# A fused S5 scan and GEGLU kernel on one core: a new hand-over order of its 692 steps

## The chip, the core and the metric

The kernel runs on one core of a Trainium2 chip. The core has five engines, each with its own instruction stream: TensorE (PE in the profile, its weight loads PEld), VectorE (DVE), ScalarE (ACT), GpSimd (POOL) and SyncE (SP), which in this kernel issues nearly all DMAs. Engines wait for each other only through semaphores. The metric is the device time of one execution in microseconds (us), and of several executions the median. Lower is better.

## The reference

The input `x` has 2048 tokens of 512 features. It is normalised, goes through a complex diagonal recurrence (S5) and, beside it, through a gated feed-forward net; the two results are multiplied and added to the input. All inputs and the output are bf16.

```python
def _A_ref(x, Lambda_re, Lambda_im, B_re, B_im, C_re, C_im, log_dt, Dskip):
    Lam = Lambda_re + 1j * Lambda_im                  # 512 states
    dt = jnp.exp(log_dt)
    Lam_bar = jnp.exp(dt * Lam)
    B_bar = ((Lam_bar - 1.0) / Lam)[:, None] * Bmat   # 512 x 512
    Bu = jnp.einsum("bld,pd->blp", x + 0j, B_bar)
    for t in range(L):                                # 2048 tokens
        h = Lam_bar[None, :] * h + Bu[:, t, :]
        hs.append(h)
    y = 2.0 * jnp.einsum("blp,dp->bld", hseq, Cmat).real + x * Dskip[None, None, :]

def _B_ref(x, w_gate, w_up, w_down):                  # 512 -> 1376 -> 512
    return (_gelu(x @ w_gate) * (x @ w_up)) @ w_down

xn = _layernorm(x, axis=-1)
s = _A_ref(xn, ...)
g = _silu(_B_ref(xn, ...))
return x + s * g
```

## The kernel before

**Tiling.** The tokens are cut into four slabs of 512, each slab into four token tiles of 128 (m = 0 to 3). The 512 features are four row tiles of 128 (k = 0 to 3), over which a matmul group accumulates in a PSUM bank. The 1376 hidden columns of the feed-forward net are cut into 512, 512 and 352 (c = 0, 1, 2). The 512 complex states are four tiles, worked on in two halves.

**What is done for a slab.** `norm` normalises it (ScalarE) and transposes it into `xnT` by a DMA. `gate_tile` (matmuls L536, ScalarE evacuations L539) makes the up and the gate products of a token tile, six groups of four matmuls; `gated` (L518, VectorE, two instructions, of 1024 and 352 columns) multiplies the two into `at`, and `at_t` transposes `at` by a DMA. `half` makes the drive of two state tiles: four groups of matmuls with `BT` (L615), evacuated by ScalarE into `U` (L617); VectorE rotates it (L627, a product over 4096 columns into `Q`), sums the products (L639, 2048 columns), runs four scans (L646) and rotates and sums back into `hst`. `down_pair` makes the down projection (L564, 11 matmuls of 512 columns a tile) and its SiLU. `y_tile` puts the skip term into a bank (L575, ScalarE), accumulates eight matmuls of `hst` with C on it (L579), multiplies by the gate (L585, `yg`), adds the input (L586, `ot`) and stores. The slabs are interleaved, so that matmuls of one slab lie beside the scans of another.

**The head.** Slab 0 is begun while weights still arrive. Its tiles are centred (L418 and L424, VectorE) and transposed on TensorE (`head_t`: L387 for tile 0 in two halves, L400 for the others, evacuated at L402 into `xcT`, which lies in the buffer `W`). Then `up_rows` (L462) multiplies one token tile with one row tile and one 512-column chunk of the up weights as soon as that piece has landed, one matmul a step; `first_w` (L499) makes a group of four matmuls, with the 352-column piece of the up weights or with the gate weights. `parameters` transposes the S5 parameters on TensorE; from them come the time step, the angles and the rotation tables.

**The loads.** SP issues them in the head one after another: the four x tiles (steps 0, 1, 2, 7; 128 KB each), the up weights in halves of a row tile (3 and 4 for row 0, 5 and 6 for row 1, 8 and 9 for row 2; 128 KB each; 10 for row 3, 256 KB), the 352-column up piece of all rows (11, 352 KB), gate columns 512 to 1375 (12, 864 KB), gate columns 0 to 511 (13, 512 KB). Behind them come x slab 1 (151), D (154), the two transposes into `BT` (14, 15, L314), slab 0's transpose into `xnT` (175, L436), the down weights (152, 1280 KB, and their 96 KB tail 153), x slabs 2 and 3 (295, 438) and the C transposes (220, 221).

**What sets the order.** The program adds 692 steps to a `Plan`, numbered as they are added, each with its engine, the steps it depends on and the buffers it holds. `Plan.run` emits them in the order of the hand-written tuple `ORDER` (L21 to L46), and the instructions are not reordered after that: each engine runs its own steps in that order, and a wait holds everything behind it on the same engine. `SLOTS` (L47 to L89) says which physical buffer or PSUM bank every group uses: `ps` are banks 0 to 5, `pp` banks 6 and 7, and the other names are the buffers of `SIZES`. The costs that the steps carry in the code are not used when the plan runs.

The steps that the prediction names, with their lines:

| steps | engine | what |
|---|---|---|
| 71 | PE | `up_rows(1, 0, 0)`, L462: first matmul of token tile 1 |
| 86, 97 / 90, 92, 94 / 101 | PE | `up_rows` of chunk 1: tile 0, rows 2 and 3 / tile 3, rows 0 to 2 / tile 1, row 3 |
| 115 | PE | `first_w` of tile 2 with the 352-column up piece, L499 |
| 129 | PE | `first_w` of tile 1 with gate columns 512 to 1023, L499 |
| 205 | PE | slab 0, `half`: first group with the second half of `BT`, L615 |
| 396; 397, 399 | PE; ACT | slab 2, `half`: first drive group; evacuations of the first two into `U` |
| 404, 405, 411 | DVE | slab 2: rotation L627, sum L639, rotation back |
| 457, 402, 609, 611, 613 | PE | groups of `gate_tile` (L536) or `half` (402, L615), each of which refills a bank |
| 483, 503, 504, 524, 525 | DVE | gated products of slab 2, L518 (503 and 524: 1024 columns) |
| 515 | ACT | evacuation of an up group, L539 |
| 507, 678 | PE | `y_tile`, L579: a slab 1 tile, and the first of slab 3 |
| 535 | DVE | `yg` product of a slab 1 tile, L585 |
| 554, 570 | DVE | slab 3: the sums that write the two halves of `hst`, L639 |

Of the kernel before, what the change touches and what calls it, by code (L numbers as in the profile page):

```python
# [18 lines left out]


ORDER = (  # L21
# [24 lines left out]
)  # L46
SLOTS = {  # L47
# [4 lines left out]
    ),  # L52
    "pp": (
        0, 1, 0, 1, 0, 1, 0, 1, 0, 0, 0, 1, 0, 1, 0, 1, 0, 1, 0, 1, 1, 0, 1, 0, 1, 1, 1, 0, 0, 0, 0, 1, 1, 0, 1, 0, 1, 0, 1,
    ),
    "U": (
        0, 1, 0, 2, 0, 1, 0, 2,
    ),
    "g2": (
        5, 0, 1, 4, 3, 0, 4, 2, 2, 0, 1, 5, 3, 1, 4, 5,  # L60
    ),
    "at": (
        2, 0, 1, 3, 2, 1, 0, 0, 0, 1, 2, 3, 2, 3, 0, 1,
    ),
    "gtA": (
        0, 0, 1, 1, 0, 1, 0, 1, 1, 0, 0, 0, 1, 1, 0, 0,
    ),
    "gtB": (
        1, 1, 0, 0, 0, 0, 1, 1, 1, 0, 0, 0, 0, 1, 0, 1,
    ),  # L70
    "ubA": (
        0, 1, 0, 0, 1, 1, 1, 0, 0, 0, 1, 1,
    ),
    "ubB": (
        0, 0, 1, 1, 1, 0, 0, 1, 0, 0, 1, 0,
    ),
    "yg": (
        0, 0, 1, 1, 0, 1, 0, 1, 0, 1, 1, 0, 0, 0, 1, 0, 1, 0,
    ),
    "ot": (  # L80
        1, 1, 1, 0, 1, 0, 0, 0, 0, 0, 0, 1, 1, 0, 1, 0, 1,
    ),
    "sk": (
        2, 3, 0, 1, 5, 7, 4, 6, 0, 1, 3, 2, 5, 4, 6, 7,
    ),
    "atT": (
        0, 1, 3, 0, 1, 1, 3, 2, 0, 3, 2, 1, 1, 2, 3, 0,
    ),
}  # L89

# [829 lines left out]
```

## Time and profile before

| | |
|---|---|
| median of 3 runs | 179.1 us (178.98 to 179.23) |
| the profiled execution, its span | 176.9 us |
| TensorE busy | 172.1 us, 97% of the span |
| VectorE busy | 154.6 us, 87% |
| ScalarE busy | 132.6 us, 75% |
| GpSimd busy | 10.9 us, 6% |
| DMA | 18.66 MB, mean 105 GB/s |
| chain that ended last | TensorE 94% of the span, DMA 2% |

The span is what the instructions of one execution cover, from the first to the last. The device time is longer by what lies around it: the median is 2.2 us above the span shown. Busy shares are averages over the whole span; the chain that ended last is followed back from the last instruction to what released each step, and tells which engine or load held the end up. A row of a view gives start and length in us, the engine, the line, the operation with its output and input buffers, the shapes, and, in brackets, how long the engine was idle just before and what released it. `SPq` is a DMA that SP has issued. An instruction's length is its own duration; on VectorE and ScalarE consecutive ones overlap a little.

### The profile page before, as it was taken

To read this page: it belongs to the slowest core of one execution; us is meant where nothing else is said; L and a number is where in the kernel's file an instruction comes from. 1 tells how busy PE (TensorE), PEld (TensorE's weight loads), DVE (VectorE), ACT (ScalarE), POOL (GpSimd) and SP (SyncE) were. 2 spreads that over 40 slices of the span, in tenths; PEclk is the share of its full clock that TensorE was granted. 3 is DMA by queue.
4 is the path that set the end of the run, shared out by engine and by line. 5 is a ranking of instruction groups with operands and counts; after the bars stand their busy time and mean duration, and the time that the engine had idled before them with its cause. 6 is when DMAs were issued, how large, how long until landed. Compare 5 with 4: busy or idle time off the path is not lost.

```text
span 176.9 us, 2418 instructions
## 1 busy us (share of the span) xinstructions
PE 172.1 (97%) x834; PEld 82.3 (47%) x849; DVE 154.6 (87%) x253; ACT 132.6 (75%) x246; POOL 10.9 (6%) x25
## 2 busy tenths in 40 slices
PE   8999999999999999999999999999999999999992
PEld 2554544454454444444444444444444444444451
DVE  3743799999999988999999699999999999999343
ACT  6679999989999999956697665735898860793310
POOL 2640500000200000011000000000000000000000
PEclk9999999999999999999999999999999999999999
DMA  5999999997092730040057050063007300550531
GB/s 150 285 347 247 160 288 189 305 217 158 8 193 43 138 62 4 0 82 0 0 115 150 2 111 0 0 126 70 0 11 154 87 0 4 129 123 0 113 119 30
DMA packets 48467, 18.66 MB, mean 105 GB/s; under 512 B 40296, under 2 KB 48328, under 8 KB 48456
## 3 DMA queue, kind: packets, MB, share of 16 engines
q1 hardware_dynamic: 48432, 18.52, 46.7%
q8 instruction: 6, 0.10, 0.2%
q14 instruction: 5, 0.04, 0.1%
q10 hardware_dynamic: 24, 0.00, 0.0%
HBM read 6.46 MB, written 2.10 MB: 48 GB/s over the span
## 4 chain that ended last, share of the span: by engine, by line
PE 94%; DMA 2%; SPq 1%; issue 1%; DVE 0%
PE bank L536 31%; PE bank L564 21%; PE bank L615 16%; PE bank L579 16%; PE bank L499 7%; PE bank L462 3%; DMA wu<-in_B_w_up_dram 2%; SPq L296 1%; SPq L287 0%; DVE yg L585 0%; DVE ot L586 0%; PE bank L400 0%
## 5 line engine op out<-in xcount | busy, mean ns | idle before, releaser
L536 PEld LDWEIGHTS <-xnT 128*128 128x128 bf16 x288 | 28.1, 98 | 29.4
L564 PE MATMUL bank<-wd,atT 128*128 128x512 bf16 (+1 forms) x174 | 40.2, 379 | 0.1
L536 PE MATMUL bank<-wu,xnT 128*128 128x512 bf16 (+1 forms) x140 | 31.9, 356 | 0.1
L536 PE MATMUL bank<-wg,xnT 128*128 128x512 bf16 (+1 forms) x139 | 31.7, 356 | 0.3
L615 PE MATMUL bank<-xnT,BT 128*128 128x512 bf16 x128 | 30.9, 379 | 0.1
L646 DVE TENSOR_TENSOR_SCAN Fs<-rho,ini,W 128x512 bf16<-128x512 f32 x24 | 29.8, 1272 | 0.1
L579 PE MATMUL bank<-C,hst 128*128 128x512 bf16 (+1 forms) x134 | 29.7, 366 | 0.1
L564 PEld LDWEIGHTS <-atT 128*128 128x128 bf16 (+1 forms) x176 | 17.2, 98 | 20.3
L539 ACT ACTIVATE ubA<-bank 128x512 bf16<-128x512 f32 x24 | 14.6, 614 | 8.8 <-PE bank L536 8.3
L617 ACT ACTIVATE U<-bank 128x512 bf16<-128x512 f32 x32 | 19.1, 622 | 1.7 <-PE bank L615 1.7
L579 PEld LDWEIGHTS <-hst 128*128 128x128 bf16 x136 | 13.3, 98 | 14.0
L615 PEld LDWEIGHTS <-BT 128*128 128x128 bf16 x128 | 12.5, 98 | 14.3
L627 DVE TENSOR_TENSOR Q<-U,tab 128x4096 bf16<-128x4096 bf16 x8 | 18.3, 2287 | 0.7 <-ACT tab L715 0.6
L539 ACT ACTIVATE gtA<-bank 128x512 bf16<-128x512 f32 x24 | 14.8, 616 | 5.3 <-PE bank L536 4.6
L627 DVE TENSOR_TENSOR Q<-Fs,tab 128x4096 bf16<-128x4096 bf16 x8 | 18.3, 2285 | 0.1
L567 ACT ACTIVATE g<-bank 128x512 f32<-128x512 f32 x16 | 9.2, 594 | 12.1 <-PE bank L564 12.1
L585 DVE TENSOR_TENSOR yg<-bank,g 128x512 bf16<-128x512 f32 (+1 forms) x17 | 11.1, 655 | 5.0 <-PE bank L579 4.6
L539 ACT ACTIVATE ubB<-bank 128x352 bf16<-128x352 f32 x12 | 5.7, 475 | 6.6 <-PE bank L536 5.5
L838 ACT ACTIVATE junk<-x_tok 128x512 bf16<-128x512 bf16 x16 | 10.2, 649 | 0.0
L499 PE MATMUL bank<-wg,W 128*128 128x512 bf16 (+1 forms) x47 | 9.7, 356 | 0.1
L843 ACT ACTIVATE xna<-x_tok,nb,rs 128x512 bf16<-128x512 bf16 x12 | 9.6, 876 | 0.0
L575 ACT ACTIVATE bank<-sk 128x512 f32<-128x512 bf16 (+1 forms) x17 | 9.5, 577 | 0.1
(121 smaller groups left out, 190.0 us busy)
## 6 DMA issues: line engine op xcount, KB each, us to landing
out_dram<-ot SPq DMA_DIRECT2D x15, 128.0 KB, 1.8
x_tok<-in_A_x_dram SPq DMA_DIRECT2D x3, 512.0 KB, 5.6
wd<-in_B_w_down_dram SPq DMA_DIRECT2D x1, 1280.0 KB, 7.1
wg<-in_B_w_gate_dram SPq DMA_DIRECT2D x1, 864.0 KB
wu<-in_B_w_up_dram SPq DMA_DIRECT2D x6, 128.0 KB, 3.3
x_tok<-in_A_x_dram SPq DMA_DIRECT2D x4, 128.0 KB, 2.2
wg<-in_B_w_gate_dram SPq DMA_DIRECT2D x1, 512.0 KB, 7.8
wu<-in_B_w_up_dram SPq DMA_DIRECT2D x1, 352.0 KB, 3.9
```

Source lines behind the costliest of these rows:

```text
L499: T.matmul(ps[:, 0 : b - a], lhsT=xcT[:, k, m * P : (m + 1) * P], rhs=wt[:, k, a:b], start=(k == 0), stop=(k == KT - 1))
L536: T.matmul(ps[:, 0 : b - a], lhsT=xnT[:, s % 2, m, k, :], rhs=wt[:, k, a:b], start=(k == 0), stop=(k == KT - 1))
L539: acts(b - a, lambda: act(out=dst, in_=ps[:, 0 : b - a], func=AF.Copy if up else AF.Gelu_apprx_tanh), [key], [ok], table=None if up else " ...
L564: T.matmul(ps[:], lhsT=atT[:fs, k, iT * P : (iT + 1) * P], rhs=wd[:fs, k, :], start=(k == 0), stop=(k == NFT - 1))
L579: T.matmul(ps, lhsT=hst[s % 2][:, j // NPT, j % NPT, m * P : (m + 1) * P], rhs=C2[:, j // NPT, j % NPT, c0:c1], start=False, stop=(j == 2 ...
L585: dve(w, lambda: V.tensor_tensor(out=yg[iy][:, 0:w], in0=ps, in1=g2[ig][:, c0:c1], op=ALU.mult), [key, ("g2", gg)], [("yg", gy)])
L615: T.matmul(ps[:], lhsT=BT[:, ri, k, pt * P : (pt + 1) * P], rhs=xnT[:, s % 2, :, k, :], start=(k == 0), stop=(k == KT - 1))
L617: acts(512, lambda q=q, ri=ri, ps=ps: act(out=U[ui][:, ri, q, :], in_=ps[:], func=AF.Copy), [key], [("U", ug, q, ri)])
L627: dve(4096, lambda: V.tensor_tensor(out=Qf, in0=src.unsqueeze(1).to_broadcast(WQ), in1=table, op=ALU.mult), reads, ["Q"], rate=2.0)
L646: pl.add(DVE, 1.12 if s == 0 else 1.185, lambda ri=ri, q=q, pt=pt, first=first: V.tensor_tensor_scan(out=Fs[:, ri, q, :], data0=rho[:, pt ...
L838: acts(512, lambda i=i, fn=fn, sc=sc, m=m: act(out=junk()[:], in_=x_tok[:, s * M + m, :], func=fn, scale=sc, accum_out=sx[:, s, i, m : m + ...
L843: acts(512, lambda m=m: act(out=xn[m], in_=x_tok[:, s * M + m, :], func=AF.Identity, scale=rs[:, s, m : m + 1], bias=nb[:, s, m : m + 1]), ...
```

## The change

The steps are the same 692, with the same work in each. What changes is `ORDER`, the order in which they are emitted, and `SLOTS`, which buffer each group uses. Both tuples are replaced as a whole.

In the head SP issues both halves of row tile 1 of the up weights (6, 5) and token tile 3 (7) ahead of the 352-column piece (11), which was issued ahead of all three. The transposes of the parameters (38) come right behind the first pair of transposes of token tile 0, and were four steps later on TensorE; their cast on VectorE (39) moves with them. TensorE's order up to the gate weights is another one. The queues, as the tuples give them:

```
SP before: 0 1 2 3 4 11 6 7 5 8 10 9 12 13 151 154 14 175 15 295 153 438 248 152 221 176 177 220 371 178
SP after:  0 1 2 3 4 6 5 7 11 8 10 9 12 13 151 154 14 175 153 15 295 248 438 177 152 220 221 176 178 179

PE before: 29 34 36 65 67 69 38 71 68 72 75 76 113 111 78 80 115 74 73 79 77 81 83 84 86 85 95 88 103
           99 97 117 89 91 105 87 93 90 101 107 92 94 129 109 139 145
PE after:  29 34 38 36 65 67 69 68 71 72 78 75 73 76 80 74 79 77 81 113 83 85 89 84 91 93 107 103 99
           111 95 88 105 87 117 129 86 121 147 127 101 90 97 119 92 94 109 137 123 135 145 143

POOL before: 28 16 62 40 63 61 64 157 155
POOL after:  16 28 40 63 62 64 157 61 155
```

The lines of the diff that hold the steps named above:

```diff
@@ -19,72 +19,72 @@
 ORDER = (
-    18, 23, 19, 17, 20, 22, 21, 29, 0, 24, 28, 16, 25, 1, 26, 2, 27, 3, 4, 30, 31, 11, 44, 32, 6, 33, 34, 46, 45, 7, 35, 5, 36, 50, 65, 47, 67, 69,
-    8, 66, 62, 38, 71, 70, 10, 39, 68, 37, 9, 72, 53, 40, 12, 13, 75, 51, 76, 113, 63, 111, 41, 114, 54, 78, 55, 80, 56, 48, 115, 57, 61, 74, 73, 79,
-    171, 77, 58, 49, 116, 52, 112, 81, 83, 42, 82, 84, 60, 86, 85, 64, 169, 95, 59, 167, 151, 154, 14, 88, 103, 99, 104, 97, 117, 173, 89, 158, 91,
-    105, 87, 93, 240, 118, 90, 101, 157, 107, 172, 236, 92, 234, 156, 94, 106, 100, 238, 129, 108, 109, 139, 237, 145, 130, 175, 241, 98, 110, 155,
-    235, 140, 174, 239, 168, 143, 102, 242, 146, 127, 128, 15, 133, 131, 121, 132, 144, 295, 243, 119, 153, 134, 120, 159, 170, 122, 246, 123, 247,
...
+    16, 28, 29, 24, 0, 1, 2, 25, 3, 26, 4, 27, 30, 44, 31, 33, 18, 32, 34, 38, 45, 36, 65, 35, 39, 67, 46, 6, 5, 7, 11, 8, 10, 9, 12, 13, 151,
+    154, 14, 50, 51, 37, 48, 47, 19, 69, 68, 66, 40, 70, 41, 55, 56, 57, 49, 71, 72, 78, 75, 73, 76, 80, 74, 79, 77, 81, 113, 63, 62, 53, 169, 17,
+    82, 83, 85, 89, 84, 91, 58, 59, 52, 114, 64, 93, 107, 108, 60, 171, 173, 54, 157, 61, 155, 167, 103, 99, 111, 112, 100, 104, 95, 88, 105, 87,
+    117, 129, 86, 130, 118, 96, 121, 147, 127, 101, 106, 156, 148, 158, 102, 240, 174, 236, 20, 238, 234, 241, 128, 122, 90, 97, 98, 119, 92, 94,
...
+    22, 219, 159, 246, 247, 244, 245, 153, 15, 199, 200, 138, 115, 131, 184, 132, 295, 248, 205, 186, 206, 187, 297, 161, 134, 185, 144, 162, 163,
...
+    276, 377, 277, 355, 375, 380, 275, 442, 345, 354, 286, 387, 395, 392, 413, 465, 455, 456, 414, 472, 473, 460, 457, 444, 447, 376, 341, 388,
+    356, 287, 474, 491, 461, 462, 512, 402, 458, 477, 464, 466, 495, 499, 500, 475, 448, 468, 291, 467, 393, 289, 383, 482, 449, 497, 520, 288,
+    290, 498, 521, 496, 403, 492, 293, 292, 381, 294, 493, 522, 523, 432, 433, 415, 398, 514, 452, 451, 513, 494, 416, 396, 397, 515, 478, 516,
+    399, 485, 518, 417, 434, 486, 450, 517, 519, 453, 382, 454, 394, 469, 418, 527, 533, 435, 404, 525, 405, 479, 528, 480, 481, 534, 524, 503,
+    409, 504, 408, 406, 407, 579, 555, 556, 483, 411, 535, 410, 412, 529, 421, 615, 609, 610, 613, 616, 532, 530, 422, 426, 536, 425, 423, 487,
+    611, 634, 612, 635, 545, 546, 614, 587, 583, 584, 588, 557, 543, 619, 617, 585, 580, 620, 618, 586, 622, 424, 427, 428, 589, 539, 540, 541,
+    598, 559, 560, 581, 632, 571, 544, 542, 590, 526, 537, 505, 484, 490, 429, 621, 488, 489, 623, 547, 582, 558, 639, 572, 633, 599, 649, 591,
+    548, 549, 538, 550, 551, 552, 553, 637, 577, 596, 578, 597, 604, 602, 561, 630, 640, 594, 506, 562, 631, 650, 507, 554, 641, 508, 563, 564,
...
+    645, 628, 629, 659, 661, 625, 654, 687, 660, 567, 566, 569, 636, 652, 642, 643, 646, 653, 638, 677, 672, 662, 655, 570, 647, 648, 682, 678,
...
 SLOTS = {
     "ps": (
-        0, 1, 2, 3, 1, 5, 4, 2, 0, 3, 2, 5, 0, 0, 5, 3, 4, 3, 5, 2, 4, 1, 4, 0, 0, 3, 2, 1, 0, 1, 0, 1, 0, 2, 2, 0, 3, 3, 0, 1, 2, 5, 4, 0, 3, 5, 4,
...
+        0, 1, 3, 2, 4, 5, 0, 1, 2, 3, 4, 2, 0, 0, 1, 3, 2, 0, 3, 0, 4, 5, 5, 5, 0, 0, 0, 3, 2, 0, 4, 1, 2, 4, 5, 2, 0, 5, 0, 4, 0, 3, 1, 5, 3,
...
```

The other pools of `SLOTS` (`pp`, `U`, `g2`, `at`, `gtA`, `gtB`, `ubA`, `ubB`, `yg`, `ot`, `sk`, `atT`) get new tuples of the same lengths. By the two orders the sequence of activation functions on ScalarE asks for 17 table loads, and for 15 before.

More of the change, by code (lines that the diff above doesn't have):

```diff
@@ L48 @@
     "ps": (
[3 rows of a table removed]
[3 rows of a table added]
     ),
     "pp": (
-        0, 1, 0, 1, 0, 1, 0, 1, 0, 0, 0, 1, 0, 1, 0, 1, 0, 1, 0, 1, 1, 0, 1, 0, 1, 1, 1, 0, 0, 0, 0, 1, 1, 0, 1, 0, 1, 0, 1,
+        0, 0, 1, 0, 1, 1, 1, 0, 0, 1, 1, 0, 0, 0, 0, 0, 0, 0, 1, 0, 1, 1, 0, 0, 1, 1, 0, 0, 1, 1, 0, 0, 1, 0, 1, 0, 1, 0, 1,
     ),
     "U": (
-        0, 1, 0, 2, 0, 1, 0, 2,
+        1, 0, 2, 1, 0, 2, 0, 1,
     ),
     "g2": (
-        5, 0, 1, 4, 3, 0, 4, 2, 2, 0, 1, 5, 3, 1, 4, 5,
+        0, 1, 2, 3, 4, 2, 0, 5, 1, 0, 5, 3, 1, 2, 4, 5,
     ),
     "at": (
-        2, 0, 1, 3, 2, 1, 0, 0, 0, 1, 2, 3, 2, 3, 0, 1,
+        2, 0, 3, 1, 0, 3, 1, 2, 2, 0, 1, 3, 3, 0, 2, 1,
     ),
     "gtA": (
-        0, 0, 1, 1, 0, 1, 0, 1, 1, 0, 0, 0, 1, 1, 0, 0,
+        1, 0, 1, 0, 0, 0, 1, 1, 0, 1, 0, 1, 0, 1, 1, 0,
     ),
     "gtB": (
-        1, 1, 0, 0, 0, 0, 1, 1, 1, 0, 0, 0, 0, 1, 0, 1,
+        1, 0, 1, 0, 1, 0, 1, 0, 1, 1, 0, 1, 1, 0, 1, 0,
     ),
     "ubA": (
-        0, 1, 0, 0, 1, 1, 1, 0, 0, 0, 1, 1,
+        0, 0, 1, 1, 1, 0, 1, 0, 1, 0, 0, 1,
     ),
     "ubB": (
-        0, 0, 1, 1, 1, 0, 0, 1, 0, 0, 1, 0,
+        1, 0, 1, 1, 0, 0, 1, 0, 1, 0, 0, 0,
     ),
     "yg": (
-        0, 0, 1, 1, 0, 1, 0, 1, 0, 1, 1, 0, 0, 0, 1, 0, 1, 0,
+        0, 0, 0, 1, 1, 0, 0, 0, 1, 1, 0, 0, 0, 1, 0, 1, 0, 1,
     ),
     "ot": (
-        1, 1, 1, 0, 1, 0, 0, 0, 0, 0, 0, 1, 1, 0, 1, 0, 1,
+        0, 1, 1, 0, 0, 0, 1, 0, 1, 1, 0, 1, 0, 1, 0, 1, 0,
     ),
     "sk": (
-        2, 3, 0, 1, 5, 7, 4, 6, 0, 1, 3, 2, 5, 4, 6, 7,
+        2, 3, 1, 0, 7, 4, 5, 6, 3, 0, 1, 2, 5, 3, 7, 6,
     ),
     "atT": (
-        0, 1, 3, 0, 1, 1, 3, 2, 0, 3, 2, 1, 1, 2, 3, 0,
+        1, 0, 2, 3, 2, 0, 3, 1, 1, 3, 0, 2, 2, 0, 1, 1,
     ),
```

33 rows, old and new, of tables (ORDER, SLOTS) are left out of this document.

## The prediction

> **What bounds the kernel now.** I read the page first (busy shares, the chain that ended last), then that chain in order of time, then the first 15 us of every engine, then the spots where TensorE is handed something with no time to spare.
>
> ```profile
> span 176.9 us, 2418 instructions
> PE 172.1 (97%) x834; PEld 82.3 (47%) x849; DVE 154.6 (87%) x253; ACT 132.6 (75%) x246; POOL 10.9 (6%) x25
> ```
>
> TensorE is the bound, and the chain tells more than the 97%:
>
> ```profile
> 3.06 3.89 DMA wu<-in_B_w_up_dram
> 6.95 0.04 issue
> 6.99 1.35 PE bank L499 x8
> 8.35 0.43 PE bank L462 x2
> 8.78 0.60 PE bank L499 x4
> 9.38 0.86 PE bank L462 x4
> 10.24 0.22 PE bank L400 x4
> ...
> 173.77 0.03 issue
> ```
>
> From 6.99, where the 352-column up piece lands, to 173.77 the chain is TensorE alone: it never waits again. A four-matmul group of 512 columns takes 0.86 (0.216 each), one of 352 columns 0.60, four transposes 0.22. The edit adds and removes no matmul, so it gains only if TensorE's gap-free stretch starts earlier with as much work done, and it loses by every wait that the new orders put into that stretch. The tail (yg, ot, the last store) has the same steps in the same order: 0.
>
> **The change, part by part.** The profiled execution spans 176.9 us; the median of the runs shown is 179.1, so 2.2 us lie outside the span and I carry them over.
>
> *The head, up to the gate weights.* TensorE of before:
>
> ```profile
> 3.90 0.66 PE L387 MATMUL bank<-ident,xna 128*128 128x128 bf16 x4
> 4.84 0.38 PE L462 MATMUL bank<-wu,W 128*128 128x512 bf16 x1
> 5.67 1.25 PE L462 MATMUL bank<-wu,W 128*128 128x512 bf16 x5
> ...
> 15.00 1.03 PE L499 MATMUL bank<-wg,W 128*128 128x512 bf16 x4
> ```
>
> and VectorE:
>
> ```profile
> 3.49 0.60 DVE L418 TENSOR_SCALAR xna<-x_tok,ma,mb 128x256 bf16<-128x256 bf16 x2
> 4.19 0.35 DVE L424 TENSOR_SCALAR xna<-x_tok,ma 128x512 bf16<-128x512 bf16 x1
> ...
> 5.07 0.42 DVE L402 COPY W<-bank 128x512 bf16<-128x512 bf16 x1
> ```
>
> In the new order VectorE makes the other half of the centred tile first, so the first transposes start 0.3 late (4.2, not 3.90); the next step waits for the centring at 4.19 anyway, and most of the 0.3 is absorbed. The cast of the transposed parameters and one memset now stand ahead of the copy at 5.07, some 0.1 together. So step 71, the first matmul of token tile 1, starts at about 5.75 instead of 5.67. The parameter loads' landing has no row. Their transposes now stand right behind the first pair, at about 4.3; had the loads landed only when the new matmuls behind them start in before (5.67), that would cost at most 1.4, of which the wait found below hides 0.6. Nothing in before waits for them, so I take 0.
>
> Behind step 71 the new order has 10 up matmuls on rows 0 and 1, the transposes of tile 3, a 352-column group, nine up matmuls, a group, four matmuls, a group: 23 x 0.216 + 0.22 + 3 x 0.60 = 6.99. TensorE would reach step 129, the first group that reads the gate weights, at 5.75 + 6.99 = 12.74. In before it got there at 15.00, with 1.90 us more done: the 352-column group of tile 2 (step 115, 0.60) and six up matmuls (86, 90, 92, 94, 97, 101: 1.30) stood ahead of it and stand behind it now. What is left at step 129 is thus 1.90 more than before, and the end is unchanged if it starts at 15.00 - 1.90 = 13.10. Unhindered, 12.74 would be a gain of 0.36.
>
> It is not unhindered. Step 129 needs the 864 KB gate piece:
>
> ```profile
> 6.45 0.98 SPq L287 DMA_DIRECT2D wg<-in_B_w_gate_dram  x2
> ```
> ```profile
> 8.92 7.26 SPq L314 DMA_TRANSPOSE BT<-in_A_B_re_dram  x1
> 16.30 3.03 SPq L436 DMA_TRANSPOSE xnT<-xna  x1
> 19.38 2.42 SPq L314 DMA_TRANSPOSE BT<-in_A_B_im_dram  x1
> ```
> ```profile
> wg<-in_B_w_gate_dram SPq DMA_DIRECT2D x1, 512.0 KB, 7.8
> wu<-in_B_w_up_dram SPq DMA_DIRECT2D x1, 352.0 KB, 3.9
> ```
> ```profile
> DMA packets 702, 0.52 MB, mean 347 GB/s; under 512 B 250, under 2 KB 702, under 8 KB 702
> ```
>
> The 512 KB gate piece, issued second at about 7.0, lands 7.8 later, at 14.8. The last line is the stretch 13.3 to 14.8: it moved 0.52 MB, just that piece. So the 864 KB piece ahead of it landed at about 13.3; at the earliest perhaps 12.7 (some of those bytes being of the loads behind), at the latest 13.5. The bytes ahead of it are the same ones in another order, so it lands then again. The pieces that change places have no landing rows at their new places. The 352 columns, now issued at about 4.6, land at 8.5 if they take 3.9 again, 0.4 after TensorE wants them (5.75 + 2.38 = 8.1); the row 1 halves, if as late as 6.95 was for the piece that had their place, stop TensorE for 0.5. Either way step 129 is reached by 13.2 at the latest, still not after the gate piece. **Step 129 starts at 13.35, not 13.10: +0.25.** Before, the same load had 1.7 us to spare.
>
> *Two more table loads on ScalarE* (17 for 15, 1.28 each) and its evacuations in another order:
>
> ```profile
> 35.00:165.00 130.00, 129.37 (x620) 61.60 (x631) 124.63 (x182) 100.74 (x181) 2.01 (x2) 1.00 0.34 69
> ```
> ```profile
> 118.63 0.60 ACT L539 ACTIVATE gtA<-bank 128x512 bf16<-128x512 f32 x1 [2.96 <-PE bank L536]
> ```
> ```profile
> 119.29 1.03 PE L615 MATMUL bank<-xnT,BT 128*128 128x512 bf16 x4
> ```
>
> From 35 to 165 (columns: stretch, then busy time of PE, PEld, DVE, ACT, POOL, then clock, DMA share, GB/s) ScalarE works 100.7 of 130 us, so 2.6 us fit. What counts is where. A bank that is filled again with one 0.86 us group in between leaves ScalarE just its own 0.60: before has one such place, at 119.29, with ScalarE idle for 2.96 just ahead, and TensorE does not wait there. The new order has four (ahead of steps 457, 402, 609, 611), each behind more than 1 us of ScalarE idleness as I add up its queue. Taken at 0; 0.1 to 0.3 each if a table load falls in.
>
> *VectorE's order.* Two races end level. Its work is spaced as follows (an instruction starts some 0.09 before the one ahead of it ends, so a start less the start before it is what one costs):
>
> ```profile
> 107.04 2.46 DVE L646 TENSOR_TENSOR_SCAN Fs<-rho,ini,W 128x512 bf16<-128x512 f32 x2
> 109.42 0.67 DVE L518 TENSOR_TENSOR at<-gtA,ubA 128x1024 bf16<-128x1024 bf16 x1
> ```
> ```profile
> 158.88 2.29 DVE L627 TENSOR_TENSOR Q<-Fs,tab 128x4096 bf16<-128x4096 bf16 x1
> 161.09 0.69 DVE L518 TENSOR_TENSOR at<-gtA,ubA 128x1024 bf16<-128x1024 bf16 x1
> 161.69 1.22 DVE L639 TENSOR_TENSOR hst<-Q 128x2048 bf16<-128x2048 bf16 x1
> 162.83 0.34 DVE L518 TENSOR_TENSOR at<-gtB,ubB 128x352 bf16<-128x352 bf16 x1
> 163.08 0.68 DVE L585 TENSOR_TENSOR yg<-bank,g 128x512 bf16<-128x512 f32 x1
> ```
> ```profile
> 164.29 5.34 PE L579 MATMUL bank<-C,hst 128*128 128x512 bf16 x24
> ```
>
> A scan costs 1.19, a rotation (Q) 2.21, a sum over 2048 columns 1.14, a gated product 0.60 or 0.25.
> Race A: step 613 (a gate product, near 117) refills the bank that step 535 (a yg product) reads. On VectorE rotation 404 waits for ScalarE's 397, 515 and 399 behind TensorE's step 396; then come 525, 405, 524, 503, four scans, 504, 483, rotation 411 and 535: 2.21 + 0.25 + 1.14 + 2 x 0.60 + 4 x 1.19 + 2 x 0.25 + 2.21 + 0.68 = 12.95. With three evacuations ahead (0.60 each, overlapping: 1.6), some 0.16 of pipeline and the hand-overs it is 14.8. TensorE has between 396 and 613 seven groups of 0.86, two of 0.60, a down projection of 11 matmuls (2.38) and three y tiles of eight (1.73): 14.8. Margin 0; I take a wait of 0.1, bounds 0 and 0.4.
> Race B: the last hidden-state half (570) has to be there for step 678, the first y tile of the last slab. Before it was done at 161.69 + 1.22 = 162.91, 1.4 ahead of 164.29. Now 554 waits for TensorE's step 507, and from there to the end of 570 VectorE has two rotations, three sums, four scans, two gated products of each size, four yg products (0.60) and four 512-column steps (0.25 to 0.60, say 0.35): 18.1, with hand-overs 18.3. TensorE has five down projections, two y tiles and four groups: 18.8. Margin 0.5, less if VectorE is a few per cent slower; I take 0.1, bounds 0 and 0.4.
>
> *SP's queue.* The 96 KB tail of the down weights goes between the xnT and the second BT transpose; the x slab 3 load goes behind the second xnT. With step 129 at 13.35 the first use of BT's second half (step 205) is at 25.9, and its transpose is issued at about 19.9 rather than 19.38. The first BT transpose, behind copies, held the queue for 7.26; this one, right behind a transpose, 2.42. The Trainium skill, DMA: Bandwidth & Descriptors, "Queues, rings and completion order", says that each engine takes descriptors in ring order and that a data descriptor is no barrier: by that rule the copy costs only its 96 KB (an estimate of some 0.3 us at 347 GB/s), and nothing waits; the 7.26 speaks for a longer hold, and then the sum would be 1.3 higher (the rival below). I take 0, because in a gap between transposes only this small copy is outstanding.
>
> **Sum:** 0.25 + 0.1 + 0.1 = 0.45; span 177.35, time 179.1 + 0.45, **179.6 us**. That is 0.25% slower; 0.2% (0.36 us) is about what a measurement of this kernel can tell from no change.
>
> **The rivals.** *Faster:* the gate piece is there by 12.7. Then step 129 starts at 12.74, 0.36 earlier in effect than its break-even, and with both races won the time is 178.7; it decides as soon as the piece lands before 13.1. For it: the rate varies from slice to slice, and nothing says that every execution moves the bytes as this one. Against: 0.52 MB after 13.3.
> *No difference:* the piece lands at 13.1 to 13.2 and both races hold, 179.1 to 179.35; the transposed parameters and the earlier row 1 then buy time that is spent again waiting. This is also the case in which the edit does not do what it says.
> *Clearly slower:* the second BT transpose is held until the 96 KB copy has landed, as the first was held for 7.26; its landing moves from 24.7 (issue 19.38 plus 5.3, the median of the xnT transposes) to about 27.2, TensorE waits 1.3 at step 205, and the time is 180.9. Against: before, the copies ahead of the first transpose were 1.5 MB still moving.
>
> ```profile
> xnT<-xna SPq DMA_TRANSPOSE x4, 5.3
> ```
>
> **How the numbers follow.** Faster rival 0.15; no difference 0.27; the sum as worked out 0.48 (its own range 179.4 to 180.0, from the bounds of the races); clearly slower 0.10. Over 0.2% slower is the last two, 0.58. The range leaves out the outer halves of the extreme cases: 178.7 to 180.5.
>
> **What would show it.** In the profile after: the first wg matmul of L499 starts near 13.35 behind a wait for the DMA, with the TensorE idle just ahead of it 0.4 to 0.6; if it starts under 13.1 without a wait, the first step is wrong. The chain has the DMA wg piece where wu stood. Race A shows as a short TensorE gap near 117 with VectorE's yg as the releaser, race B as one near 165 behind hst. A gap near 25.9 ended by BT would be the last rival. The prediction fails most cheaply if the gate piece lands half a microsecond earlier.

## The result: 0.4 to 0.55% slower, inside the range that was forecast

The changed kernel takes 179.75 us (median of 8, 179.40 to 181.36) where the kernel before takes 178.95 (8 runs beside it, 178.40 to 179.23): ratio 1.0055, 95% interval 1.0033 to 1.0078. A second comparison of the same two gave 179.59 to 179.01, 1.0042 (1.0025 to 1.0059). The prediction was 179.6, in a range of 178.7 to 180.5, against 179.1 for the kernel before: 0.25% slower.

The execution profiled first is the slowest of the 15 (181.36), and its profile shows something that the prediction did not think of. The page of the changed kernel:

```profile
span 179.6 us, 2420 instructions
...
PE 174.4 (97%) x833; PEld 83.3 (46%) x849; DVE 154.5 (86%) x253; ACT 135.5 (75%) x248; POOL 13.0 (7%) x25
```

and two rows of TensorE's timeline in it (start, length, engine, line, what, count):

```profile
6.47 4.33 PE L462 MATMUL bank<-wu,W 128*128 128x512 bf16 x11
...
10.87 0.76 PE L499 MATMUL bank<-wu,W 128*128 128x352 bf16 x4
```

Eleven up matmuls at 0.216 each would take 2.54 (ten spacings and the 0.38 of the last); they took 4.33. Most of them were spaced by 0.427, as the warming matmuls on constants are at the start: TensorE ran at half its rate until 10 us. A second execution (179.58, close to the median) is the one to read. Its span and the head of its TensorE:

```profile
span 177.8 us, 2436 instructions
```
```profile
4.21 0.40 PE L387 MATMUL bank<-ident,xna 128*128 128x128 bf16 x2 [0.31 <-DVE xna L418]
...
4.87 0.63 PE L400 MATMUL bank<-ident,xna 128*128 128x128 bf16 x4
...
6.14 2.81 PE L462 MATMUL bank<-wu,W 128*128 128x512 bf16 x11
...
9.08 0.76 PE L499 MATMUL bank<-wu,W 128*128 128x352 bf16 x4
...
13.08 0.76 PE L499 MATMUL bank<-wu,W 128*128 128x352 bf16 x4
13.67 0.59 PE L499 MATMUL bank<-wg,W 128*128 128x512 bf16 x2
```

The bracket tells how long the engine was idle before and for what. The first transposes start 0.3 late, the last row is step 129, and it follows the group ahead of it without a wait.

One number makes the two orders comparable although they do the same work in another sequence. I call it the **lead lost** at a step: its start, less the work at full rate that TensorE has to do ahead of it, the warming matmuls not counted (0.2157 a 512-column matmul, 0.1493 a 352-column one, 0.0555 a transpose, 0.06 for the parameters; spacings as the trace has them). It only grows where TensorE waits or runs slowly. At step 113, the first group with the 352-column piece, before had three tiles' transposes, the parameters and six up matmuls behind it, 0.66 + 0.06 + 1.30 = 2.02, and started at 6.99: 4.97 lost. The changed kernel has four tiles' transposes and twelve up matmuls, 0.88 + 0.06 + 2.59 = 3.53 (3.54 without rounding), and starts at 9.08: 5.54, so in these two executions **0.57 of the time is lost by step 113**. At the end of the chain TensorE stops here:

```profile
172.88 1.76 PE bank L579 x16
174.64 0.02 issue
```

174.64 against 173.77 before: 0.87 in all, between these two executions. (The medians are 0.58 and 0.80 apart; the section after the experiments comes back to it.) The other 0.30 is lost in two places. At 117, with TensorE and VectorE in one timeline:

```profile
116.71 1.03 PE L536 MATMUL bank<-wu,xnT 128*128 128x512 bf16 x4
116.96 0.68 DVE L585 TENSOR_TENSOR yg<-bank,g 128x512 bf16<-128x512 f32 x1
...
117.69 1.02 PE L536 MATMUL bank<-wg,xnT 128*128 128x512 bf16 x4
```

This is the prediction's race A. Step 609 starts at 116.71 and its four spacings end at 117.57; step 613 starts at 117.69, just behind the end of step 535 on VectorE (116.96 + 0.68 = 117.64), whose bank it refills: 0.12 late. And at 153:

```profile
150.82 0.58 ACT L539 ACTIVATE ubA<-bank 128x512 bf16<-128x512 f32 x1
151.30 0.46 ACT L539 ACTIVATE ubB<-bank 128x352 bf16<-128x352 f32 x1
151.77 1.28 ACT L539 ACT_TABLE_LOAD   x1
...
153.06 0.60 ACT L539 ACTIVATE gtA<-bank 128x512 bf16<-128x512 f32 x1
...
153.71 0.74 PEld L564 LDWEIGHTS <-atT 128*128 128x128 bf16 x4 [0.27 <-issue]
```

A GELU evacuation (step 601) has to wait for its table load, and a down projection (step 573) for the bank that it empties; its weights are loaded as soon as the evacuation ends (153.06 + 0.60). The two down projections in TensorE's own timeline:

```profile
151.18 5.07 PE L564 MATMUL bank<-wd,atT 128*128 128x512 bf16 x22
```

22 matmuls without a pause would take 21 x 0.2157 + 0.38 = 4.91; they took 5.07, so 0.16 is lost between the two. 0.57 + 0.12 + 0.16 = 0.85 of the 0.87.

### The profile page after: what moved, and what is told of

Its sections match the earlier page's. It is cut to its first block, busy times and chain, and to the rows that moved or that the text cites. A ratio compares the mean times of both kernels' runs of the same rounds, so it can differ in the third digit from the quotient of the medians.

```text
span 179.6 us, 2420 instructions
## 1 busy us (share of the span) xinstructions
PE 174.4 (97%) x833; PEld 83.3 (46%) x849; DVE 154.5 (86%) x253; ACT 135.5 (75%) x248; POOL 13.0 (7%) x25
## 4 chain that ended last, share of the span: by engine, by line
PE 95%; DMA 2%; issue 1%; DVE 1%; ACT 0%; SPq 0%
PE bank L536 31%; PE bank L564 21%; PE bank L579 15%; PE bank L615 15%; PE bank L499 7%; PE bank L462 5%; DMA x_tok<-in_A_x_dram 2%; PE bank L400 1%; DVE yg L585 0%; ACT junk L423 0%; SPq L296 0%; DVE xna L424 0%; DVE ot L586 0%
## 5 line engine op out<-in xcount | busy, mean ns | idle before, releaser
L564 PE MATMUL bank<-wd,atT 128*128 128x512 bf16 (+1 forms) x171 | 39.7, 379 | 0.3
L536 PE MATMUL bank<-wg,xnT 128*128 128x512 bf16 (+1 forms) x142 | 32.8, 356 | 0.2
L615 PE MATMUL bank<-xnT,BT 128*128 128x512 bf16 x128 | 31.4, 379 | 0.0
L579 PEld LDWEIGHTS <-hst 128*128 128x128 bf16 x136 | 13.3, 98 | 14.2
L539 ACT ACTIVATE gtA<-bank 128x512 bf16<-128x512 f32 x24 | 14.4, 608 | 3.1 <-PE bank L536 2.6
L499 PE MATMUL bank<-wg,W 128*128 128x512 bf16 (+1 forms) x47 | 10.2, 356 | 0.1
L462 PE MATMUL bank<-wu,W 128*128 128x512 bf16 x31 | 9.9, 457 | 0.0
```

Source lines behind the costliest of these rows:

```text
L462: T.matmul(ps[:], lhsT=xcT[:, k, m * P : (m + 1) * P], rhs=wu[:, k, a:b], start=(k == 0), stop=(k == KT - 1))
L499: T.matmul(ps[:, 0 : b - a], lhsT=xcT[:, k, m * P : (m + 1) * P], rhs=wt[:, k, a:b], start=(k == 0), stop=(k == KT - 1))
L536: T.matmul(ps[:, 0 : b - a], lhsT=xnT[:, s % 2, m, k, :], rhs=wt[:, k, a:b], start=(k == 0), stop=(k == KT - 1))
L539: acts(b - a, lambda: act(out=dst, in_=ps[:, 0 : b - a], func=AF.Copy if up else AF.Gelu_apprx_tanh), [key], [ok], table=None if up else " ...
L564: T.matmul(ps[:], lhsT=atT[:fs, k, iT * P : (iT + 1) * P], rhs=wd[:fs, k, :], start=(k == 0), stop=(k == NFT - 1))
L579: T.matmul(ps, lhsT=hst[s % 2][:, j // NPT, j % NPT, m * P : (m + 1) * P], rhs=C2[:, j // NPT, j % NPT, c0:c1], start=False, stop=(j == 2 ...
```

## The experiments

Each edit is of `ORDER` only, or of the number of warming matmuls; buffers were assigned anew where two orders were joined or banks moved. Theory 1 in the expectations is the prediction's (the gate piece is late at step 129, and the races cost a little each); theory 2 puts the loss down to the half rate of the first matmuls. Where a text speaks of the piece, it is the 352-column piece of the up weights (step 11). The comparisons are with the kernel before, run beside them (178.86 to 179.09).

**The changed kernel once more.** No edit.

> The changed kernel once more, for a second profile and more times. Theory 1 (the prediction's): step 129 waits 0.4 to 0.6 for the gate piece, matmuls in front of it run at 0.216 each from about 5.7, and the times lie 0.3 to 0.6 above before, close together. Theory 2 (half rate): the first profiled execution spaced its matmuls by 0.427 until 10.0 us, where before switched to 0.216 at 4.6; if that is what costs, the switch lies at another place in each execution, the time moves by half of the time spent at the slow spacing after 5.7 (up to 2.2), and executions spread by more than 1 us while those of before, which waits until 6.95 anyway, do not.

Measured: 179.59 (7 runs, 179.34 to 180.22), the profile above. Neither theory as it stood: step 129 does not wait, which is against theory 1, and the slow spacing lasts a little past 6 us, 0.27 in the row of eleven. A third reading comes out of it, theory A in the later expectations: what counts is when the 352-column piece lands against the work in front of it. Theory B there is theory 2.

**Step 129 later.**

```diff
-    ... 87, 117, 129, 86, 130, 118, 96, 121, 147, 127, 101, 106, ... 122, 90, 97, 98, ...
+    ... 87, 117, 86, 97, 101, 129, 130, 118, 96, 121, 147, 127, 106, ... 122, 90, 98, ...
```

> The changed kernel with the up matmuls 86, 97 and 101 (0.216 each) taken in front of step 129, so that 129 is reached 0.65 later. Theory 1: the wait for the gate piece (0.4 to 0.6) is filled, 0.25 to 0.6 faster than the changed kernel, 178.7 to 179.3. Theory 2: no wait is there to be filled in slow-starting executions, so less than 0.2 of difference.

Measured: 179.78 (179.39 to 179.95), ratio 1.0042 (1.0029 to 1.0055). No gain: there was no wait to be filled, and theory 1's largest term falls. Its TensorE at step 113:

```profile
8.87 0.76 PE L499 MATMUL bank<-wu,W 128*128 128x352 bf16 x4 [0.20 <-DMA wu<-in_B_w_up_dram]
```

Here TensorE was at full rate earlier than in the execution above, and waited for the 352-column piece until 8.87: lead lost 8.87 - 3.54 = 5.33. The chain that ended last has the piece landing at 8.83, 4.34 after its issue:

```profile
4.49 4.34 DMA wu<-in_B_w_up_dram
```

**Head and rest exchanged.** The new order up to step 129 with the old order behind it, and the other way round.

```diff
-ORDER = <changed kernel>
+ORDER = <changed kernel up to 129> + <before, without those steps>
```
```diff
-ORDER = <before>
+ORDER = <before up to 129> + <changed kernel, without those steps>
```

> The changed kernel's order up to and with step 129, then the steps that are left in the order of the kernel before. Theory 1: the head costs 0.25 of the loss, the races in the middle 0.2: about 179.2 to 179.3. Theory 2: the whole loss is in the head, so it costs as much as the changed kernel, 179.7.

> The order of the kernel before up to and with step 129, then what is left in the changed kernel's order. Theory 1: only the races are left, 179.1 to 179.5. Theory 2: nothing is left of the loss, 178.8 to 179.1.

Measured: 180.57 (180.48 to 180.69) and 179.88 (179.62 to 180.24). As totals they tell nothing, because the joints make waits of their own; the view of waits of the first, and two views of TensorE and its weight loads in the second:

```profile
PE bank L462 <- ACT at L471: 0.9, 1, 0.9
```
```profile
117.07 1.03 PE L536 MATMUL bank<-wu,xnT 128*128 128x512 bf16 x4
118.05 1.02 PE L536 MATMUL bank<-wg,xnT 128*128 128x512 bf16 x4
```
```profile
154.06 2.04 PEld L564 LDWEIGHTS <-atT 128*128 128x128 bf16 x10 [0.27 <-issue]
```

The 0.9 is a bank that ScalarE empties late at the joint. What can be read: the new rest carries its two waits with it behind the old head too (117.07 + 0.863 = 117.93, next start 118.05: 0.12 again; and the same 0.27 ahead of the down projection's weights). They belong to the rest and not to how late the head is. With the old rest behind the new head, neither is there.

**Only the loads moved, in the kernel before.**

```diff
-    ... 3, 4, 30, 31, 11, 44, 32, 6, 33, 34, 46, 45, 7, 35, 5, ...
+    ... 3, 4, 30, 31, 6, 5, 7, 11, 44, 32, 33, 34, 46, 45, 35, ...
```

> The kernel before with only the loads moved: steps 6, 5 and 7 are issued ahead of 11. Theory A (what counts is when the 352-column piece lands against the full-rate work that stands in front of its first group): the piece lands near 8.85, as in the last profiles, with 2.02 us of work in front instead of the 3.54 of the changed kernel; TensorE stands still from about 6.8 to 8.85 and everything behind is 1.9 later than in before, 180.9. Theory B (what costs is the time that TensorE runs at the slow spacing): no more than 0.3 over before, 179.0 to 179.3.

Measured: 180.95 (180.15 to 181.49), ratio 1.0107 (1.0079 to 1.0135), 2.1 more than before. The wait is where theory A has it, in the slowest of the four executions (181.49), in which the piece came near 9.7 and not near 8.85:

```profile
9.77 1.35 PE L499 MATMUL bank<-wu,W 128*128 128x352 bf16 x8 [2.53 <-DMA wu<-in_B_w_up_dram]
```

Moving the loads alone costs 2.1. The new order of TensorE's steps is what wins 1.3 to 1.5 of it back (it puts 1.52 more in front of step 113).

**The loads moved back, in the changed kernel.**

```diff
-    ... 46, 6, 5, 7, 11, 8, 10, 9, ...
+    ... 46, 11, 6, 7, 5, 8, 10, 9, ...
```

> The changed kernel with the loads in the order of before (11, 6, 7, 5). Theory A: no wait at the 352-column group (piece there at 7.0); instead step 78, which needs step 6's half with 1.37 of work in front of it, waits until 7.3, a lead lost of 5.94 against 5.5 in the changed kernel: about 0.4 over it, 180.0. Theory B: same as the changed kernel, 179.6 to 179.8.

Measured: 180.46 (180.21 to 180.84), 0.7 to 0.85 over the changed kernel, where 0.4 was expected. The place is right (step 78), the landing was later than I had taken it:

```profile
6.02 0.81 PE L462 MATMUL bank<-wu,W 128*128 128x512 bf16 x3
7.80 2.15 PE L462 MATMUL bank<-wu,W 128*128 128x512 bf16 x8 [0.97 <-DMA wu<-in_B_w_up_dram]
```

The two halves of the change belong together: each without the other is slower than the two together.

**Fewer and more warming matmuls.** In the changed kernel 4 and 8 instead of 7, in the kernel before 4.

```diff
-    dummies(7)
+    dummies(4)
```

> The changed kernel with 4 warming matmuls on constants at the start instead of 7 (they make nothing that is used), so that TensorE stands still from about 2.4 to 4.1. Theory B: the slow spacing of 0.427 goes on until 6 to 10 us, and each matmul after 5.5 that has it costs 0.21: 0.5 to 2.2 over the changed kernel, 180.2 to 181.8. Theory A alone: the 352-column piece hides up to 0.4 of that, and if the spacing does not depend on what TensorE did before, nothing changes, 179.6 to 179.8.

> The changed kernel with 8 warming matmuls instead of 7: TensorE is busy until about 4.1, right up to the first transposes. Theory A (the landing of the 352-column piece sets the head): the piece lands at 8.85 all the same, and the time is that of the changed kernel less at most 0.2, 179.5 to 179.8. Theory B (the slow spacing sets it): it ends earlier, the executions lie closer together (none above 180.0) and the median is 0.2 to 0.4 lower, 179.3 to 179.5.

> The kernel before with 4 warming matmuls instead of 7. If its wait for the 352-column piece until 6.95 hides a late change of spacing, it loses 0.3 us less than the changed kernel did by the same edit (0.75): 179.1 to 179.4. If it hides nothing, it loses as much: 179.6 to 179.8.

Measured: the changed kernel with 4 takes 180.46 (180.20 to 181.03), with 8 179.75 (179.63 to 180.12); before with 4 takes 179.88 (179.29 to 180.43), ratio 1.0052 (1.0034 to 1.0070). In this order, their TensorE, and for the one with 8 the row of the chain that ends its wait:

```profile
6.09 3.79 PE L462 MATMUL bank<-wu,W 128*128 128x512 bf16 x11
...
9.94 0.76 PE L499 MATMUL bank<-wu,W 128*128 128x352 bf16 x4
```
```profile
5.80 2.53 PE L462 MATMUL bank<-wu,W 128*128 128x512 bf16 x11
...
9.17 0.76 PE L499 MATMUL bank<-wu,W 128*128 128x352 bf16 x4 [0.55 <-DMA wu<-in_B_w_up_dram]
```
```profile
4.49 4.63 DMA wu<-in_B_w_up_dram
```
```profile
6.15 2.31 PE L462 MATMUL bank<-wu,W 128*128 128x512 bf16 x5
8.25 1.81 PE L499 MATMUL bank<-wu,W 128*128 128x352 bf16 x8
```

With 4, the row of eleven takes 3.79 (1.26 over full rate) and step 113 starts at 9.94, with no wait. One such row proves little, as 7 gave 4.33 in the first execution and 2.81 in the second; the times carry it: all four executions with 4 lie at 180.20 or above, of the fifteen with 7 just two do. So the rate depends on what TensorE did before, and a late change of it costs the changed kernel 0.7 to 0.9. With 8, all eleven are at full rate (2.53), and it gains nothing: TensorE waits 0.55 for the 352-column piece, until 9.17, no earlier than the 9.08 of the second execution. **That settles the head**: the piece is a floor under it (8.87 - 3.54 = 5.33 and 9.17 - 3.54 = 5.63 lost at step 113 in the two profiles that wait for it here), and the slow spacing comes on top only where it lasts longer than the piece takes to land, as in the first profile. Theory B's 0.2 to 0.4 for this kernel failed. Before does not hide a late change either: in its profile with 4, the slowest of the six, its five matmuls took 2.31 where 1.25 is the full rate, and its median lost 0.97.

**Row 2 ahead of the piece, and two small repairs.**

```diff
-    ... 31, 33, 18, 32, 34, ... 6, 5, 7, 11, 8, 10, ... 81, 113, ... 83, 85, 89, 84, ... 627, 603, 601, ...
+    ... 31, 32, 33, 18, 34, ... 6, 5, 7, 8, 11, 10, ... 81, 83, 85, 84, 113, ... 89, ... 601, 627, 603, ...
```

> The changed kernel with four repairs: step 8 (a half of row tile 2) loaded ahead of the 352-column piece and its matmuls 83, 85, 84 in front of step 113; step 32 ahead of 33 on VectorE, so that the first transposes start near 3.9; step 601 (a GELU evacuation) ahead of 627 and 603, so that its table load starts as soon as the SiLU is through and step 573 does not wait 0.15 for its bank. Theory A: the piece lands near 9.25 with 4.19 in front, a lead lost of 5.06 against 5.33 to 5.5, and with the 0.15 the time is 0.4 to 0.6 under the changed kernel, 179.0 to 179.3. Theory B: only the 0.15 and what the earlier start gives, 179.4 to 179.6.

Measured: 179.61 (11 runs, 178.78 to 180.15), ratio 1.0040 (1.0023 to 1.0056): not the 179.0 to 179.3 expected.

At step 113, and around the evacuation 601:

```profile
9.64 0.76 PE L499 MATMUL bank<-wu,W 128*128 128x352 bf16 x4 [0.34 <-DMA wu<-in_B_w_up_dram]
```
```profile
150.82 1.28 ACT L539 ACT_TABLE_LOAD   x1
...
151.10 3.62 PE L564 MATMUL bank<-wd,atT 128*128 128x512 bf16 x16
...
152.12 0.60 ACT L539 ACTIVATE gtA<-bank 128x512 bf16<-128x512 f32 x1
```

The one more load put the piece back to 9.6, later than the 9.25 I had expected, with 4.18 in front: 5.46 lost. So 0.65 of work in front was paid for with a landing some 0.5 to 0.8 later than the 9.12 and 8.83 above. The table load's repair did what it was to do: step 601's table load starts at 150.82 and not at 151.77, the evacuation ends at 152.72, and sixteen matmuls of the down projections, the eleven of the first and five of the second, take 3.62 (15 x 0.2157 + 0.38), without the pause between them. A gain of 0.16 is too small to show in these times, but the pause is gone in the trace, and that shows its cause.

**The piece last.** The order of the loads is 6, 5, 7, 8, 10, 9, 11; TensorE takes 113 behind 95, and 111 behind 88. The two small repairs of the run above (32 ahead of 33 on VectorE, 601 ahead of 627 on ScalarE) are in it too.

```diff
-    SP: 6 5 7 11 8 10 9      PE: 81 113 83 85 89 84 91 93 107 103 99 111 95 88 105 87 117 129
+    SP: 6 5 7 8 10 9 11      PE: 81 83 85 84 89 91 93 107 103 99 95 113 88 111 105 87 117 129
```

> The changed kernel with the 352-column piece loaded last of the up weights (order 6, 5, 7, 8, 10, 9, 11) and its groups moved behind matmuls of rows 2 and 3 (113 behind 95, 111 behind 88), and with step 32 ahead of 33 and 601 ahead of 627. Theory A: no wait for the piece, which lands near 10.9 and is wanted at 11.1 at the earliest, so the lead lost at step 113 is 4.8 to 5.0 in place of 5.33 to 5.54, and the table load's 0.15 is gone: 178.9 to 179.2, level with before or better. Theory B: what the first matmuls lose by the slow spacing stays, 179.3 to 179.6.

Measured: 179.78 (179.56 to 180.18), ratio 1.0053 (1.0039 to 1.0068). The wait for the piece is smaller, and others have come with it:

```profile
9.45 1.68 PE L462 MATMUL bank<-wu,W 128*128 128x512 bf16 x7 [0.15 <-DVE W L402]
11.13 0.76 PE L499 MATMUL bank<-wu,W 128*128 128x352 bf16 x4
...
13.50 0.76 PE L499 MATMUL bank<-wu,W 128*128 128x352 bf16 x4 [0.37 <-ACT at L471]
```

The seven matmuls at 9.45, which wait for a copy on VectorE, would leave TensorE ready for step 113 at 9.45 + 7 x 0.2157 = 10.96; it starts at 11.13, 0.04 behind the last landing mark of the piece (11.09), so the piece holds it up by 0.17 even with ten more matmuls in front. Step 117 refills a bank that ScalarE has not emptied yet: the 352-column groups stand close together, and two banks take turns for them. At step 117 7.53 stands in front, 13.50 - 7.53 = 5.97 lost.

**Half of the change, on the kernel before.** Only step 6 goes ahead of the piece, with its three matmuls.

```diff
-    SP: 3 4 11 6 7 5      PE: 72 75 76 113 111 78 80 115 74 73 79 77 81
+    SP: 3 4 6 11 7 5      PE: 72 75 76 78 80 77 113 111 74 115 73 79 81
```

> The kernel before with a third of the load change and matmuls to go with it: only step 6 (one half of row tile 1) is issued ahead of the 352-column piece, and its three matmuls 78, 80 and 77 (0.65) are taken in front of step 113; 74 goes ahead of 115. Theory A: the piece lands 0.4 later, near 7.35, and TensorE is ready for it at 7.2 to 7.6 with 2.67 in front, so the lead lost at step 113 is 4.7 to 4.9 in place of 4.97: 0.1 to 0.25 faster than before, 178.7 to 178.8. Had any load put ahead of the piece to be paid in full (0.4 to 0.5 each, as the changed kernel pays for three), it would be slower, 179.1 to 179.4.

Measured: 179.21 against 179.09 (11 and 14 runs), ratio 1.0016 (1.0001 to 1.0032): level, or a little slower. The head did what theory A says, and the gain was spent 3 us later:

```profile
5.62 1.90 PE L462 MATMUL bank<-wu,W 128*128 128x512 bf16 x8
7.36 1.36 PE L499 MATMUL bank<-wu,W 128*128 128x352 bf16 x8
...
10.27 0.38 PE L400 MATMUL bank<-ident,xna 128*128 128x128 bf16 x4 [0.27 <-ACT at L471]
```
```profile
9.66 0.55 ACT L471 ACTIVATE at<-bank,rs 128x352 bf16<-128x352 f32 x1 [0.30 <-POOL rs L366]
```

Step 113 starts at 7.36 with 0.66 + 0.06 + 9 x 0.2157 = 2.66 in front: 4.70 lost in place of 4.97, no wait. But the transposes of tile 3 (step 81) need a bank that an evacuation ending at 10.21 holds, which itself waited for GpSimd's scale factors: 10.27 less 5.11 of work is 5.16 lost. No version here beats the kernel before.

## Why the prediction was right, and where it was not

**The sign and the range held, and the number is close by luck.** Its largest term, 0.25 for a wait at step 129, is not there in the profiles. In its place stands a loss ahead of step 113, where the prediction had none. Point by point:

- *What bounds the kernel.* Right. TensorE is gap-free from the head to 174.64 but for the two short pauses, and the difference of the ends is the sum of what the head and the pauses lose.
- *The head, step 71 at about 5.75.* This step failed. In the second execution the first transposes were 0.31 late as forecast, but "most of the 0.3 is absorbed" was not so, and the transposes and first matmuls ran at half rate (0.63 instead of 0.40 a group). Step 71 began at 6.57: the row at 6.14 begins with step 68, and 0.427 later comes step 71.
- *The 352-column piece, "land at 8.5 if they take 3.9 again".* This step failed too. The mechanism was named and its size missed: it landed at 8.83 and 9.12 in the two profiles of this head whose chain runs through it (step 129 later, 8 warming matmuls; 4.34 and 4.63 after its issue at 4.49). "Either way step 129 is reached by 13.2 at the latest" rested on it; 129 was reached at 13.67.
- *Step 129 waits for the gate piece, +0.25.* Wrong: no wait in any profile of this head, and filling it gained nothing. In the second execution the gate piece also came earlier than I had taken it. By the method of the prediction, in the second execution's view of the DMAs:

```profile
DMA packets 600, 0.57 MB, mean 380 GB/s; under 512 B 51, under 2 KB 600, under 8 KB 600
```
```profile
wg<-in_B_w_gate_dram SPq DMA_DIRECT2D x1, 512.0 KB, 7.4
```

  The first line is the stretch 12.9 to 14.4: the 512 KB piece, landing at 14.35 (issued at 6.94), and little more, so the 864 KB ahead of it were there by about 12.9 and not at 13.3. That is one execution. The trace holds, for every DMA, the marks by which its parts report that they have landed, sixteen for these loads, and by the last one the 864 KB came at 13.38 in before, as the prediction read it, and in the changed order at 12.91 here, 13.98 in the first execution and 13.63 with 8 warming matmuls, where step 129 started at 13.76. So its landing was read rightly, but it differs by 1.1 between executions, and what kept its wait out of the time is that TensorE came later still. Had TensorE been on time at 12.74, it would have waited 0.15 in this execution and the kernel would have been faster by some 0.2 by the break-even of 13.10, the condition of the faster rival (under 13.1). That rival lost to the head and the 352-column piece, which I had costed as hidden behind the gate wait.
- *Race A, +0.1.* Right in place and size: 0.12 at 117.57. The cause agrees by its timing, a start 0.05 behind the end of step 535 on VectorE; no run here takes that race away.
- *Race B, +0.1.* Not lost. The last hidden-state half ended at 164.88, and TensorE came to the first tile that uses it later, at 163.43 + 1.73 = 165.16 (step 655's tile goes ahead):

```profile
163.67 1.21 DVE L639 TENSOR_TENSOR hst<-Q 128x2048 bf16<-128x2048 bf16 x1
```
```profile
163.43 7.07 PE L579 MATMUL bank<-C,hst 128*128 128x512 bf16 x32
```

  The row is four y tiles without a break. The margin of 0.5 was about 0.3, and it was enough.
- *Two more table loads, 0.* Mis-sized: one table load costs 0.16. Whether it is one of the two that the change adds, the profiles do not tell. The text had "0.1 to 0.3 each if a table load falls in", and looked for it ahead of steps 457, 402, 609 and 611; it fell ahead of step 573, where the order of ScalarE puts two copies in front of the GELU. The groups of table loads, before and after:

```profile
L567 ACT ACT_TABLE_LOAD x7 | 9.0, 1283 | 0.1
L539 ACT ACT_TABLE_LOAD x6 | 7.7, 1283 | 0.1
```
```profile
L567 ACT ACT_TABLE_LOAD x8 | 10.3, 1283 | 0.1
L539 ACT ACT_TABLE_LOAD x7 | 9.0, 1283 | 0.1
```

- *SP's queue, 0, and the clearly slower rival.* Right. The second transpose into BT was issued with the small copy ahead of it and held for 3.01, and the first group that uses it runs inside a row without a wait:

```profile
18.25 0.63 SPq L763 DMA_DIRECT2D wd<-in_B_w_down_dram  x1
18.93 3.01 SPq L314 DMA_TRANSPOSE BT<-in_A_B_im_dram  x1
```
```profile
25.36 2.75 PE L615 MATMUL bank<-xnT,BT 128*128 128x512 bf16 x12
```

So the sum was 0.25 + 0.1 + 0.1 = 0.45 in the text and 0.57 + 0.12 + 0.16 = 0.85 in the profiles; the medians differ by 0.58 and 0.80. "Slower by more than 0.2%" was right. The reason behind it, that the new order has to wait for its weights, was right with the wrong weights named, and it left out that the first matmuls could be slow.

The 0.85 and the medians are not the same comparison. In every run with both figures the device time is 1.7 to 1.9 above the span. So the execution of before that is shown, span 176.9, took about 178.7, some 0.3 under its median, and the 2.2 that were carried over as lying outside the span were too much by 0.4; that shifts no difference. The 0.12 at 117 and the 0.16 at 153 are in every profile with the new rest, apart from the 0.16 where it was repaired. That leaves 0.3 to 0.5 of the medians' difference for the head, and the 0.57 is the head of two executions.

Piece or half rate? By the last of its landing marks the piece came at 9.04 in the second execution, and step 113 starts 0.04 behind that, as in before (6.95 and 6.99). The last transpose ahead of it starts at 8.96, so TensorE was ready at 9.01. There the piece alone makes 0.57, and the late and slow first steps alone would have made 0.50. In the first execution the piece came at 8.96 and step 113 starts at 10.87: there it is the half rate. With 4 warming matmuls the piece came at 8.15 and step 113 starts at 9.94. In an execution like the second, taking away one of the two gains little while the other stands, as the run with 8 shows. What stays open is how the two share the loss in the executions that have no profile.

## What to carry to other kernels

For each load in the head, set its landing against the work that stands in front of its first user; a load that moves back by three places has to get as much work in front as it lands later, and a wait found behind it is no cover for a mistake ahead of it. Before an early matmul is costed at its full rate, look at the spacing of the matmuls ahead of it, and in more than one execution. A landing read from one profile is one draw: the same loads in the same order came up to 1.6 us apart. Where ScalarE changes its table between a copy and an evacuation, ask which bank waits, and put the evacuation that frees it first.

## What the runs showed of the hardware

TensorE's first matmuls run at half rate (0.427 apart for 512 columns, 0.216 later), and when that changes differs between executions of one kernel: the same eleven matmuls took 4.33 in one and 2.81 in the other. What TensorE did before counts: in the eleven profiles with seven warming matmuls the last matmul at half rate starts between 2.8 and 6.2 us in ten and at 9.5 in one; in the two with four it starts at 7.8 and 8.8. The granted clock that the profile lists was 1.00 and 0.999 for the two executions and does not show it. The Trainium skill, TensorE: Matmul & The Clock Gate, "Part 1: The HAM clock gate (the "warmup" mystery)", says that the array starts at half its clock and is let go after a busy window of about 3.4 us that runs free of the kernel. The spacings and the scatter agree with it; the window itself no run here shows.

Putting loads ahead of another one cost it more than their bytes. With three loads or 384 KB ahead of it that were behind it before, the 352-column piece landed at 8.15 to 9.73 in seven profiles (mean 9.0), and at 6.95 to 7.65 in the four that load in the order of before (mean 7.3): 1.7 later, where 384 KB at the 380 GB/s of the gate pieces' stretch are 1.0. Most of it is the issue, which moved from 3.06 to 4.49, as SP issues one load behind the other (0.43 each and a little between them). A fourth load of 128 KB (0.35) ahead of it went with a landing at 9.6; that is one execution, and lies inside the scatter.
